# The order of a fused attention and Fourier-mixing kernel: a list scheduler's order replaced by a stored table

## The chip, the core and the metric

The kernel runs on one core of one Trainium2 chip. The metric is the device time of one execution in microseconds (us), as the median of three runs. The kernel before takes 950.33 us (949.66 to 951.9). Beside these runs stands one profiled execution with its trace; its durations are used in the working.

The core has five queues that run side by side, each strictly in its own order: the tensor engine (PE, with its weight loads PEld), the vector engine (DVE), the scalar engine (ACT), GpSimd (POOL) and the queue that issues most DMAs (SP). A step waits on semaphores for what it reads and for the buffers it writes, and everything behind it on its queue waits with it.

## What is computed

```
# q, k, v: 8 batches, 8 heads, 576 tokens, 64 wide; heads 0-3 a local mask (32 back), heads 4-7 a strided mask (every 32nd)
scores = scale * q @ k.T ; masked ; softmax ; attn @ v          -> x: [8, 576, 512]
X = fft(fft(x, axis=1), axis=2)
u = x + real(X)
un = (u - mean(u)) / sqrt(var(u) + 1e-6)                         # over the last axis
out = u + relu(un @ w_ch1) @ w_ch2                               # 512 -> 2048 -> 512
```

## The kernel before, in words

The work is cut into short steps written as Python generators (called threads here). A step yields an `op`: the engine it belongs to, an estimated duration, the buffers it takes and gives back (`get`, `put`) and the events it needs and sets. The class `Order` holds all open threads and picks, one after the other, the step that its cost model lets start first, with a priority (`bias`) for each kind of thread; then it lets that thread emit its instructions. So the result of `Order` is nothing but an order: the sequence in which instructions are put on each queue. Some steps may run on more than one engine (`alt`); `Order` chooses the engine too. While the two weight matrices are being read, `self.fill` puts small dummy matmuls on PE where the model sees a gap. `run` is called twice, once for the start (first batch of the attention, reading of the first weights) and once for the rest.

The threads, with the names used below (`b` is a batch, `hp` a pair of heads, so `5_2` is batch 5, pair 2; the pairs come in the order 2, 0, 1, 3):

- **Attention** (`att_pair`, lines 407 to 530): `load` (SP, L415 and L418), `sq` (ACT, L425 to L427, sums of squares of what was loaded), `total` (PE, L359), `scales` (DVE), `hi` and `lo` (ACT L446, DVE L461: split into two float16 halves), `vhi`, `vlo`, `scores` (PE, L484), `weigh`, `max`, `sub` (DVE, L813, L820, L822), `exp` (ACT), `wlo` (DVE, L500), `turn` (SP, a DMA transpose, L503), `pv` (PE, L515 or L522), `out` (DVE, L837 on), `xd` (SP, store to DRAM). Pairs 0 and 1 are local (tile `qk`), 2 and 3 strided (tile `pbt`).
- **Fourier mixing** (`fft_batch`), once per batch when its four `xd` have landed: `xa` (SP, a load, L893) and `xb` (POOL, four indirect gathers, L897), `O` and `E` (POOL, DVE, L907), `cosa` to `cosf`, `sin`, `SD`, `FH`, `FL` (split halves, ACT L920 and DVE L924 and L925), then the PE steps `A0`, `A2`, `A3` (L1015) with their evacuations `AH` (ACT, L1023) and `AL` (DVE, L1028), and `B0`, `B1`, `B2` (L1038) with `pq`, `rt`, `u`. `fcm` and the like come from `fscale`.
- **The two matrix products**, in 18 chunks `c` of 256 tokens: `st`, `rstd`, `un`, `uhi`, `ulo`, `uT` (normalise, split, transpose by DMA), eight `up c.n` (PE, L1387, 24 matmuls each), each followed by `relu c.n` (ACT, L1403 and L1404, tile `hb`, and `hf`, of which there is one) and `hlo c.n` (POOL, L1406), and eight `down c.n` (PE, L1427, 12 matmuls each, two half steps for n = 0), then two `fin c` (DVE, L1437), which free the two accumulators, and `store`. A `down c.n` needs `hlo c.n`; four hidden buffers go round.
- **The last three chunks** (15 to 17, class `Folded`) use sums of weight blocks. These are made in advance by `fold` (DVE, L1481), `fhi` (ACT, L1485) and `flo` (DVE, L1488, L1490) once the attention is over. Their PE steps are L1571 (`up`, `up2`, `up3`, `up4`) and L1714 (`down`), their vector steps `y11` (L1609), `y22`, `y12` (L1648), `s1` to `s4` (L1658), `hlo` (L1684).

PE runs two streams interleaved: the large `up` and `down` steps of one or two chunks, and between them the small steps of attention and Fourier mixing for later batches. The small PE results go to two PSUM buffers `big`, the `up` results to two buffers `ph`, the `down` results to two accumulators.

Of the kernel before, what the change touches and what calls it, by code (L numbers as in the profile page):

```python
# [19 lines left out]
B, H, S, D = 8, 8, 576, 64  # L20
# [3 lines left out]
    c=12.731, z=13.906, f0=-24.028, w0=-22.847, s0=-1.359, w1=3.314, s1=-5.983, p0=-26.912, p1=4.962, pn=-4.352,  # L24
# [141 lines left out]
class Op:  # L166
# [3 lines left out]
    def __init__(self, engine, dur, get="", put="", need="", sets="", at=None, lat=None, n=1, slack=0.0, dma=0.0, note="", alt=None):  # L170

        self.alt = {engine: (dur, 0.0), **{e: d if isinstance(d, tuple) else (d, AL) for e, d in alt.items()}} if alt else None
        self.engine, self.dur, self.at, self.n, self.slack, self.dma, self.note = engine, dur, at, n, slack, dma, note
        self.get = [g for g in get.split() if g[0] != "-"]

        self.put = put.split() + [g[1:] for g in get.split() if g[0] == "-"]
        self.need, self.sets = need.split(), sets.split()
        self.room = [(g, self.get.count(g)) for g in dict.fromkeys(self.get)]
        self.blocked = 0
        w = note.split()[0] if note else ""  # L180
        self.port = not w.startswith(PORT)
        self.lat = lat if lat is not None else {"S": 1.6, "T": 0.15}.get(engine, 0.1)


WT = {e: P["W" + e] for e in "SVAGT"}


class Order:


    def __init__(self):
        self.threads, self.free, self.room, self.events = [], dict.fromkeys("TVAGSDQ", 0.0), {}, {}
        self.waits = {}
        self.now = 0.0
        self.fill = None
        self.lock = 0.0, 0.0
        self.ring = []

    def free_events(self, e):
        self.events[e] = self.now  # L200
        for w in self.waits.pop(e, ()):
            w.blocked -= 1

    def spawn(self, gen, bias=None, at=None):
        th = [gen, self.bias if bias is None else bias, self.now if at is None else at, None]
        self.step(th, None)

    def step(self, th, end):
        try:
            o = th[3] = th[0].send(end)  # L210
            for e in o.need:
                if e not in self.events:
                    o.blocked += 1
                    self.waits.setdefault(e, []).append(o)
            if th not in self.threads:
                self.threads.append(th)
        except StopIteration:
            if th in self.threads:
                self.threads.remove(th)

    def run(self, part=False):
        while self.threads:
            best, cand = None, []
            for th in self.threads:
                o = th[3]
                if o.blocked:
                    continue
                t = th[2] if o.at is None else o.at
                ok = True
                for g, k in o.room:  # L230
                    r = self.room[g]
                    if len(r) < k:
                        ok = False
                        break
                    if r[k - 1] > t:
                        t = r[k - 1]
                if not ok:
                    continue
                for e in o.need:
                    if self.events[e] > t:  # L240
                        t = self.events[e]
                if o.alt:
                    o.engine = min(o.alt, key=lambda e: max(t, self.free[e]) + o.alt[e][0] + o.alt[e][1])
                    o.dur = o.alt[o.engine][0]
                est = max(t + o.slack, self.free[o.engine])
                if o.engine == "V" and o.port and o.dur and self.lock[0] <= est < self.lock[1] - 0.1:
                    est = self.lock[1] - 0.1
                if o.engine == "S" and o.dur:

                    est = max(est, self.free["D"] - 2.0)  # L250
                if o.engine == "A" and o.dma and len(self.ring) > 7:
                    est = max(est, self.ring[-8])
                cand.append((est, th))
                if best is None or est < best[0]:
                    best = est, o.engine
            if best is None and part:
                return
            if best is None:
                raise RuntimeError("stuck: " + str([(th[3].note, th[3].get, [e for e in th[3].need if e not in self.events]) for th in self.threads]))

            est, th = min((c for c in cand if c[1][3].engine == best[1] and c[0] <= best[0] + WT[best[1]]), key=lambda c: (c[1][1], c[0]))
            o = th[3]
            if o.engine == "T" and self.fill:
                n = int((est - self.free["T"] - 0.3) / 0.11)
                if n > 2:
                    self.fill(n)
            if o.engine == "S" and o.dur:
                self.free["S"] = est + 0.5 * o.n
                at = max(est + 1.3, self.free["D"])
                both = min(o.dur, max(0.0, self.free["Q"] - at))  # L270
                end = self.free["D"] = max(at + o.dur + both, est + 0.42 * o.n + 1.1)
                self.free["Q"] += both
            else:
                end = self.free[o.engine] = est + o.dur
                if o.engine == "G" and o.port and o.dur:
                    self.lock = est, end
                if o.dma and o.engine == "A":
                    at = max(est + 1.3, self.free["Q"])
                    both = min(o.dma, max(0.0, self.free["D"] - at))
                    end = self.free["Q"] = at + o.dma + both  # L280
                    self.free["D"] += both
                    self.ring.append(end + 1.3)
                elif o.dma:
                    end = self.free["D"] = max(est + 2.0, self.free["D"]) + o.dma
            for g in o.get:
                self.room[g].pop(0)
            self.now = th[2] = end + (o.lat if o.dur else 0)
            self.bias = th[1]
            self.step(th, self.now)
            for g in o.put:  # L290
                self.room[g] = sorted(self.room[g] + [self.now])
            for e in o.sets:
                self.events[e] = self.now
                for w in self.waits.pop(e, ()):
                    w.blocked -= 1


op = Op
# [3 lines left out]
def body(ctx: ExitStack, tc: tile.TileContext, a, out):  # L302
# [103 lines left out]
    def att_pair(b, hp):  # L406
# [41 lines left out]
        def values():  # L448
# [7 lines left out]
            V.scalar_tensor_tensor(out=lo, in0=src, scalar=sc[0:vp, 2:3], in1=hi, op0=ALU.mult, op1=ALU.subtract)  # L456

        spawn(values())
        yield op("V", 1.6, at=end - 0.65, put="" if local else "qk", note=f"lo {nm}")
        for hi, lo, src, f in parts:  # L460
            V.scalar_tensor_tensor(out=lo, in0=src, scalar=f, in1=hi, op0=ALU.mult, op1=ALU.subtract)  # L461
        if local:

            pb = qk.bitcast(F16)[:, 0 : 2 * NQB * 128].rearrange("p (x g c) -> p x g c", x=2, c=128)

            def pad():
                yield op("G", 0.5, sets=f"pad{nm}", note=f"pad {nm}")
                G.memset(pb[:, :, :, WIN:], 0.0)

            spawn(pad())  # L470
        else:
            pb = pbt
# [63 lines left out]
    def attended(b, hp):  # L536

        left.discard((b, hp))
        if left:
            return  # L540
        apool.release()
        pool = tail["pool"] = tc.alloc_tile_pool(name="tail", bufs=1, side="right", reuse_waits="tile")
        t = pool.tile([128, 25088], F16, name="tail")
        tail[0] = t[:, 0:16384].rearrange("p (n x d c) -> p n x d c", n=16, x=2, d=2)
        tail["t"] = t
        tail["hop"] = [hop(0), hop(1)]
        S_.room["hop"] = [S_.now] * 2
        tail["uTx"] = [t[:, 23552:25088].rearrange("p (n c) -> p n c", c=128)]
        S_.free_events("tail")
        S_.room["uTx"].append(S_.now)  # L550
        for q in range(4):
            spawn(folds(0, q), bias=P["tp"] + 0.1 * q)
            spawn(folds(1, q), bias=P["tp"] + 0.1 * q + 0.05)
# [1335 lines left out]
```

## Time and profile before

| | |
|---|---|
| runs | 950.33 us median of 3 (949.66 to 951.9) |
| profiled execution, first to last instruction | 946.9 us |
| PE busy | 910.9 us (96%) |
| DVE busy | 717.0 us (76%) |
| ACT busy | 506.2 us (53%) |
| POOL busy | 343.5 us (36%) |
| share of TensorE's full clock granted, mean | 0.986 |

The profile gives the span of the profiled execution and no separate time for it; the median of the runs lies 3.4 us above the span. A busy share is a sum over the whole span. Matmuls are pipelined, so PE counts as busy over short holes; a wait of PE is listed only where it stood idle. Times of day in the rows are us from the first instruction.

### The profile page before, as it was taken

Reading aid. Unit: us, or ns where it says so; the run is one execution under the profiler, and the core shown is the slowest. Engines: PE = TensorE matmul, PEld = TensorE weight load, DVE = VectorE, ACT = ScalarE, POOL = GpSimd, SP = SyncE. Lnnn points to the kernel's source line nnn. Section 1 sums busy time; section 2 is a strip of 40 time slices with the busy share of each in tenths; the row PEclk is TensorE's granted clock in tenths of the full one; section 3 lists DMA queues with packets and bytes.
Section 4 is the critical chain, followed back from the end, with each engine's and each line's share of the span. In section 5 each row is a group of like instructions: output and inputs, shape, how many; then the busy total and the mean of one; then the engine's idle time right before and its main releaser. Section 6 shows DMA issues by size and latency. Waiting matters only on the chain.

```text
span 946.9 us, 25320 instructions
## 1 busy us (share of the span) xinstructions
PE 910.9 (96%) x10597; PEld 668.4 (71%) x10599; DVE 717.0 (76%) x1342; ACT 506.2 (53%) x987; POOL 343.5 (36%) x315
## 2 busy tenths in 40 slices
PE   8778999999899999999999999999999999999997
PEld 6656885766666667665766677676666766689996
DVE  5988875678783896747956966697679889788675
ACT  4848874554653655643746564646423444365452
POOL 0240332245353631335325522552246256334000
PEclk9969999999999999999999999999999999999999
DMA  9788485363335635584445524625240102021100
GB/s 320 243 327 276 136 217 164 121 174 56 92 89 132 151 81 107 105 156 102 117 88 169 116 86 100 173 73 145 44 125 1 45 7 56 18 52 24 41 24 24
DMA packets 140371, 108.41 MB, mean 114 GB/s; under 512 B 108256, under 2 KB 118752, under 8 KB 140256
## 3 DMA queue, kind: packets, MB, share of 16 engines
q1 hardware_dynamic: 137696, 98.40, 38.7%
q0 software_dynamic: 2560, 8.39, 3.0%
q8 instruction: 83, 1.36, 0.6%
q14 instruction: 32, 0.26, 0.1%
HBM read 64.26 MB, written 18.89 MB: 88 GB/s over the span
## 4 chain that ended last, share of the span: by engine, by line
PE 77%; DMA 8%; DVE 7%; issue 3%; POOL 2%; ACT 2%; SPq 1%; DVEq 0%; POOLq 0%; ACTq 0%
PE acc L1427 28%; PE ph L1387 27%; PE acc L1714 5%; PE f L1571 2%; PE B L1038 2%; DMA xb<-xd,ridx 2%; DMA q<-in_w 2%; PE A L1015 1%; PE s L484 1%; DVE fold L1481 1%; PE o L515 1%; DMA W<-in_w 1%; DMA vn<-in_vl 1%; PE f_0x L1571 1%; DMA q<-in_qk 1%
## 5 line engine op out<-in xcount | busy, mean ns | idle before, releaser
L1387 PE MATMUL ph<-uT,W 128*128 128x256 f16 x2880 | 329.3, 273 | 1.2 <-DMA uT<-hb 1.2
L1387 PEld LDWEIGHTS <-W 128*128 128x128 f16 x2880 | 277.4, 98 | 42.8 <-DMA uT<-hb 1.4
L1427 PE MATMUL acc<-W,hb 128*128 128x512 f16 x1344 | 302.6, 379 | 1.5 <-DVE ub L1437 1.5
L1406 POOL TENSOR_TENSOR hb<-hf,hb 128x512 f16<-128x512 f32 x112 | 160.7, 1435 | 279.0 <-ACT hb L1404 196.5
L1427 PEld LDWEIGHTS <-hb 128*128 128x128 f16 x1344 | 129.2, 98 | 143.8 <-issue 1.7
L1403 ACT ACTIVATE hf<-ph 128x512 f32<-128x512 f32 x120 | 71.2, 593 | 180.7 <-PE ph L1387 113.1
L1404 ACT ACTIVATE hb<-ph 128x512 f16<-128x512 f32 x112 | 66.2, 591 | 0.0
L1481 DVE TENSOR_TENSOR fold<-fold,W 128x512 f32<-128x512 f32 x64 | 52.4, 847 | 0.3
L1714 PEld LDWEIGHTS <-tail 128*128 128x128 f16 x504 | 48.3, 98 | 5.3
L461 DVE SCALAR_TENSOR_TENSOR kt<-qk,sc,kt 128x576 f16<-128x576 f32 (+1 forms) x40 | 37.7, 982 | 3.3 <-ACT kt L446 3.1
L907 POOL TENSOR_TENSOR O<-xa,xb 128x1536 f32<-128x1536 f32 x8 | 33.5, 4189 | 16.0 <-DMA xb<-xd,ridx 12.4
L1161 POOL TENSOR_TENSOR rstd<-mv,negh 128x1 f32<-128x1 f32 x30 | 21.7, 730 | 44.0 <-DVE mv L1158 39.5
L1571 PEld LDWEIGHTS <-tail 128*128 128x128 f16 x576 | 34.7, 98 | 2.6 <-issue 1.4
L1658 POOL TENSOR_TENSOR hb<-hb 128x256 f32<-128x256 f32 x13 | 12.2, 950 | 65.4 <-DVE hb L1658 64.3
L1714 PE MATMUL acc<-fold,tail 128*128 128x256 f16 x288 | 35.0, 273 | 0.0
L446 ACT ACTIVATE kt<-qk,sc 128x576 f16<-128x576 f32 (+1 forms) x40 | 29.3, 784 | 10.1 <-DVE sc L402 9.0
L1140 ACT ACTIVATE pq<-B,fcm 128x128 f32<-128x128 f32 (+7 forms) x105 | 27.3, 380 | 11.5 <-PE B L1038 6.3
L1684 DVE TENSOR_TENSOR tail<-hb,tail 128x512 f16<-128x512 f32 (+1 forms) x47 | 31.8, 704 | 1.9 <-ACT tail L1681 1.5
L1681 ACT CAST tail<-hb 128x512 f16<-128x512 f32 (+1 forms) x48 | 25.6, 563 | 9.1 <-DVE hb L1658 5.5
L1179 DVE TENSOR_TENSOR unp<-un,unp 128x512 f16<-128x512 f32 x28 | 22.6, 806 | 9.1 <-ACT unp L1176 9.1
L1028 DVE SCALAR_TENSOR_TENSOR AT<-A,AT 128x290 f16<-128x290 f32 (+3 forms) x35 | 15.1, 479 | 18.8 <-ACT AT L1023 17.1
L897 POOL DMA_INDIRECT xb<-xd,ridx x24 | 26.7, 1111 | 7.3 <-issue 6.1
(313 smaller groups left out, 1550.9 us busy)
## 6 DMA issues: line engine op xcount, KB each, us to landing
qk<-in_qk SPq DMA_DIRECT2D x28, 592.0 KB
sa<-in_w SPq DMA_DIRECT2D x19, 512.0 KB
out<-ub SPq DMA_DIRECT2D x32, 256.0 KB
vn<-in_vl SPq DMA_DIRECT2D x10, 432.0 KB
W<-in_w SPq DMA_DIRECT2D x8, 512.0 KB
xd<-xo SPq DMA_DIRECT2D x16, 256.0 KB
xa<-xd SPq DMA_DIRECT2D x8, 512.0 KB
vn<-in_vs SPq DMA_DIRECT2D x10, 384.0 KB
```

The source lines that it names most:

```text
L446: A.activation(hi, src, AF.Copy, scale=f)
L461: V.scalar_tensor_tensor(out=lo, in0=src, scalar=f, in1=hi, op0=ALU.mult, op1=ALU.subtract)
L907: tt_ = lambda e, o, x, y, op: e.tensor_tensor(out=o, in0=x, in1=y, op=op)
L1387: T.matmul(ph[:, i, :], W1[:, 4 * (f0 // 512) + d, x, f0 % 512 : f0 % 512 + 128], self.uhl[y][:, d, :], start=(n == 0), stop=(n == 11))
L1403: A.activation(hf, ph, AF.Relu, scale=HS)
L1404: A.activation(hh, ph, AF.Relu, scale=HS)
L1406: G.tensor_tensor(out=hl, in0=hf, in1=hh, op=ALU.subtract)
L1427: T.matmul(self.acc[s], (hh, hl)[x][:, i, 128 * s : 128 * s + 128], W2[:, f, 1 - y, :], start=(f == 0 and n == 0), stop=(f == 15 and n == 2))
L1481: on(e).tensor_tensor(out=w, in0=w if x is None else x, in1=y, op=ALU.add if f else ALU.subtract)
L1571: T.matmul(dst[:, 128 * f : 128 * f + 128], w(x, i)[:, 128 * f : 128 * f + 128], u(y, i), start=opens and f == 0 and n == 0, stop=closes a ...
L1684: on(o).tensor_tensor(out=lo, in0=src, in1=hi, op=ALU.subtract)
L1714: T.matmul(dst, hop[:, x, j, 128 * i : 128 * i + 128], w(y, i), start=bank not in opened, stop=q == 3 and z in (6, 5, 3, 4) and i == 1 and ...
```

## The change

The list scheduler goes. `FIRST` and `SECOND` hold, for the two calls of `run`, the number of the thread that takes its next step (two digits in base 36), `SIDES` the engine for each step that has a choice, and `FILL` how many dummy matmuls stand before which step. The generators, and with them every instruction, its operands and its buffers' sizes, stay as they are.

```diff
+FIRST = (
+    "000m00000000000001000102000102000103020004040302050004030d060705030d060708060e0905080e09050f080a0a0d0f08080d0a0b"
...
+SECOND = (
+    "212424241g1h1i1j1g231l1g1h0r1o1g1i1h1g1h1x1i1i1j0r3z1h421l1i0r421j40441l1j1l451l1o1j431x1m461o47481x4b1o3z1k1n48"
...
+SIDES = (
+    "VVAVVAVAVVAAGVGVVGGAVVAVVAAVAVAVVAVAAVAAVAVAVAAVAAVVVAVAVAVVVVVAVVAAGVVGVGVVVVVVVVVVVVVVGVVGVGVVVVVVVGVVVVVVVVVV"
...
+FILL = {
+    8: 49, 17: 3, 39: 6, 47: 6, 55: 9, 63: 8, 70: 3, 77: 20, 85: 7, 89: 7, 103: 38, 119: 25, 124: 6, 162: 136, 263:
+    47, 415: 3, 1119: 6, 2148: 11
+}
...
     def spawn(self, gen, bias=None, at=None):
-        th = [gen, self.bias if bias is None else bias, self.now if at is None else at, None]
+        th = [gen, None]
+        self.threads.append(th)
         self.step(th, None)
...
-            est, th = min((c for c in cand if c[1][3].engine == best[1] and c[0] <= best[0] + WT[best[1]]), key=lambda c: (c[1][1], c[0]))
...
+        t = next(self.tables)
+        for i in range(0, len(t), 2):
+            th = self.threads[int(t[i : i + 2], 36)]
+            if th[1].alt:
+                th[1].engine = next(self.sides)
+            if self.fill and self.count in FILL:
+                self.fill(FILL[self.count])
+            self.count += 1
+            self.step(th, 0.0)
```

Read out by the generators, the two orders have the same 2,573 steps. `FIRST` is the list scheduler's order, every step with a choice has the engine it had, and the 370 dummy matmuls stand where they stood. What differs are places on the queues. Counted as what lies outside the longest common sequence, these are 68 of 551 steps on PE, 155 of 852 on DVE, 88 of 605 on ACT, 35 of 234 on POOL and 35 of 249 on SP. In the trace of before the first of them stands at 148 us and the last at 850 us. The places that the text below speaks of:

```
PE, batch 2   before: up 2.6, scores 3_0, up 2.7, A0 2, A2 2, down 2.4, A3 2, up 3.0
              after:  down 2.4, scores 3_0, up 2.6, up 2.7, A0 2, down 2.5, A2 2, up 3.0, A3 2
DVE           before: weigh 3_0, FL257 2, max 3_0, sub 3_0, AL0 2      after: weigh 3_0, max 3_0, sub 3_0, AL0 2, FL257 2
PE, batch 5   before: up 6.0, up 6.1, down 5.6, pv 4_1, scores 5_2, up 6.2, down 5.7, up 6.3, down 6.0, down 6.1, total 5_0,
                      up 6.4, up 6.5, down 6.2, pv 5_2, scores 5_0, up 6.6, down 6.3, down 6.4, up 6.7, down 6.5, up 7.0, down 6.6, pv 5_0
              after:  up 6.0, pv 4_1, up 6.1, down 5.6, scores 5_2, down 5.7, up 6.2, down 6.0, up 6.3, down 6.1, total 5_0,
                      down 6.2, up 6.4, up 6.5, up 6.6, pv 5_2, scores 5_0, down 6.3, down 6.4, up 6.7, down 6.5, up 7.0, down 6.6, pv 5_0
ACT           before: relu 6.2, exp 5_2, sq 5_0, relu 6.3               after: exp 5_2, sq 5_0, relu 6.2, relu 6.3
POOL          before: hlo 6.2, xb 4, hlo 6.3, O 4, hlo 6.4, hlo 6.5     after: xb 4, hlo 6.2, hlo 6.3, hlo 6.4, hlo 6.5, O 4
SP            before: uT 7_0, uT 7_1, xd 4_1, load 5_0, xa 4, turn 5_2  after: xd 4_1, uT 7_0, xa 4, load 5_0, uT 7_1, turn 5_2
PE, batch 6   before: up 8.4, up 8.5, pv 6_2, scores 6_0, down 8.2, down 8.3
              after:  down 8.2, down 8.3, up 8.4, scores 6_0, pv 6_2, up 8.5
POOL          before: O 5, hlo 8.4, pad 6_0                              after: hlo 8.4, pad 6_0, O 5
SP            before: xd 6_2, load 6_1, turn 6_0                         after: turn 6_0, xd 6_2, load 6_1
DVE, fin 13   before: fold, fold, fold, fold, fin 13, fin 13            after: fold, fold, fin 13, fold, fin 13, fold
DVE, chunk 15 before: hlo 15.0, hlo 15.0, y11 15.1                       after: hlo 15.0, y11 15.1, hlo 15.0
              before: ulo 16.3, fold, y12 15.1                           after: fold, ulo 16.3, y12 15.1
```

## Rows read from the trace of the kernel before

**Rows 1.** The page: the span, and busy time of each engine.
```profile
span 946.9 us, 25320 instructions
...
PE 910.9 (96%) x10597; PEld 668.4 (71%) x10599; DVE 717.0 (76%) x1342; ACT 506.2 (53%) x987; POOL 343.5 (36%) x315
```
**Rows 2.** Busy time by stretch: length, PE, PEld, DVE, ACT, POOL, granted clock, DMA, GB/s.
```profile
40.00:80.00 40.00, 32.54 (x290) 23.83 (x290) 33.27 (x56) 20.80 (x34) 15.24 (x11) 0.74 0.79 284
530.00:760.00 230.00, 230.00 (x2444) 160.22 (x2442) 180.91 (x331) 116.89 (x240) 88.51 (x83) 1.00 0.35 91
780.00:795.00 15.00, 14.77 (x112) 10.78 (x111) 14.80 (x18) 6.37 (x11) 10.67 (x10) 1.00 0.10 24
810.00:820.00 10.00, 10.00 (x76) 6.96 (x75) 6.26 (x10) 3.95 (x7) 2.31 (x2) 1.00 0.01 2
```
**Rows 3.** Waits of PE: line, releaser, us in total, times, longest.
```profile
PE A L1060 <- DVE FD L907: 5.5, 1, 5.5
...
PE o L522 <- DMA pT<-pbt: 3.1, 2, 2.2
...
PE acc L1427 <- DVE ub L1437: 1.5, 1, 1.5
...
PE f L1571 <- DVE raw L1609: 0.7, 1, 0.7
...
PE f_2x L1571 <- ACT raw L1619: 0.4, 1, 0.4
```
**Rows 4.** The chain that ended last: start, us, what.
```profile
250.45 2.62 PE ph L1387 x24
...
254.95 2.59 PE acc L1427 x12
```
**Rows 5.** Timeline, 241 to 254 us: start, us, instructions, idle before.
```profile
243.37 0.88 DVE L924 SCALAR_TENSOR_TENSOR FH<-O,fsc,FH 128x510 f16<-128x510 f32 x1 [0.22 <-ACT FH L920]
...
247.38 1.15 ACT L1023 ACTIVATE AT<-A 65x290 f16<-65x290 f32 x3
...
249.23 0.38 PE L1015 MATMUL A<-csin,FH 128*127 128x145 f16 x3 [2.69 <-DVE AT L1028]
```
**Rows 6.** Timeline, 404 to 432 us.
```profile
409.82 0.43 SPq L418 DMA_DIRECT2D vn<-in_vl  x1
...
416.88 1.16 ACT L427 ACTIVATE jk<-vn 96x1152 f16<-96x1152 f32 x1 [0.20 <-DMA vn<-in_vl]
...
419.23 1.15 POOL L1406 TENSOR_TENSOR hb<-hf,hb 128x512 f16<-128x512 f32 x1 [2.23 <-issue]
...
419.86 5.40 PE L1387 MATMUL ph<-uT,W 128*128 128x256 f16 x48
...
430.03 1.76 DVE L907 TENSOR_TENSOR E<-xa,xb 128x1536 f32<-128x1536 f32 x1 [3.62 <-DMA xb<-xd,ridx]
...
430.07 0.78 PE L522 MATMUL o<-vsx,pT 54*64 54x65 f16 x72 [2.21 <-DMA pT<-pbt]
```
**Rows 7.** Timeline, 436 to 452 us.
```profile
436.95 0.60 ACT L1403 ACTIVATE hf<-ph 128x512 f32<-128x512 f32 x1 [11.99 <-POOL hb L1406]
...
438.63 2.02 DVE L822 TENSOR_TENSOR sm<-sm,mx 128x864 f32<-128x864 f32 x1
...
450.32 1.06 PE L515 MATMUL o<-vlx,pT 96*64 96x65 f16 x54 [0.42 <-DMA pT<-qk]
```
**Rows 8.** Timeline, 787 to 798 us.
```profile
790.10 5.47 DVE L1481 TENSOR_TENSOR fold<-fold,W 128x512 f32<-128x512 f32 x4
...
795.50 1.40 DVE L1437 SCALAR_TENSOR_TENSOR ub<-acc,cout,ub 128x512 f32<-128x512 f32 x2
```
**Rows 9.** Timeline, 832 to 846.5 us.
```profile
833.82 2.19 DVE L1684 TENSOR_TENSOR tail<-hb,tail 128x512 f16<-128x512 f32 x2
...
843.34 0.43 DVE L1546 TENSOR_TENSOR unp<-un,unp 128x256 f16<-128x256 f32 x1 [1.25 <-ACT unp L1543]
843.68 0.68 DVE L1481 TENSOR_TENSOR fold<-W 128x512 f32<-128x512 f16 x1
```

More of the change, by code (lines that the diff above doesn't have):

```diff
@@ new lines @@
+SIDES = (
+    "VVAVVAVAVVAAGVGVVGGAVVAVVAAVAVAVVAVAAVAAVAVAVAAVAAVVVAVAVAVVVVVAVVAAGVVGVGVVVVVVVVVVVVVVGVVGVGVVVVVVVGVVVVVVVVVV"
+    "GVGVVGVVVVVVVVVVVVVVVVVGVVGVGVVVVVVVVVVVVVVVVVGVVGVGVVVVVVVVVVVVVVVVVGVGVVGVVVVVVVVVVVVVVVVVVVVVVVVVVVVGVVVVGVVV"
+    "VGVVVVVVVVVVVVVVVVVVVVVVVVVVVVVVVVVVVVVVGVVVVVVVVVGGGGVGGVVVVVVVVVGVVVVVVVVGVVGVVVGVVGGGVVVGVVVVVVGVVVVVVVVVGVGV"
+    "VGVGVVGVGVGVGVVVGVVVVVGVVGGVVVVVGVVVVVVVVVVVVVVVVVVVVVVVVVVVVVVVVGVVVVVVVGVVVVVVVGV"
+)
+FILL = {
+    8: 49, 17: 3, 39: 6, 47: 6, 55: 9, 63: 8, 70: 3, 77: 20, 85: 7, 89: 7, 103: 38, 119: 25, 124: 6, 162: 136, 263:
+    47, 415: 3, 1119: 6, 2148: 11
+}
@@ L188 @@
 class Order:
     def __init__(self):
[L192 to L197, printed above, removed]
+        self.threads, self.free, self.room, self.now, self.fill, self.count = [], dict.fromkeys("TVAGSDQ", 0.0), {}, 0.0, None, 0
+        self.tables, self.sides = iter((FIRST, SECOND)), iter(SIDES)
     def free_events(self, e):
-        self.events[e] = self.now
@@ L201, in free_events @@
-        for w in self.waits.pop(e, ()):
-            w.blocked -= 1
+        pass
     def spawn(self, gen, bias=None, at=None):
-        th = [gen, self.bias if bias is None else bias, self.now if at is None else at, None]
+        th = [gen, None]
+        self.threads.append(th)
         self.step(th, None)
@@ L209, in step @@
         try:
[L210 to L216, printed above, removed]
+            th[1] = th[0].send(end)
         except StopIteration:
-            if th in self.threads:
-                self.threads.remove(th)
+            th[1] = None
     def run(self, part=False):
[L222 to L259, printed above, removed]
-            est, th = min((c for c in cand if c[1][3].engine == best[1] and c[0] <= best[0] + WT[best[1]]), key=lambda c: (c[1][1], c[0]))
[L262 to L295, printed above, removed]
```

47 lines of the change are left out of this document (added).

## The prediction

> **What bounds the kernel now.** I read the page first. The span is 946.9 us and PE is busy for 910.9 us of it, 96%; the next engine, DVE, stands at 76% [rows 1]. The table by stretches says what that means for an order: between 530 and 760 us PE is busy for 230.00 of 230.00 us at full granted clock [rows 2]. A change that adds and removes no instruction cannot gain there. It can only take out time in which PE stands still, so the view that decides is the list of what PE waits for [rows 3], and the timelines around each of those waits. The largest entry, 5.5 us before A0 of the first batch (L1060), and the waits on the first weights lie before 148 us, where the first moved step stands; they stay. In the stretch of the moves, 148 to 850 us, PE is idle for more than 0.15 us at seven places only:
>
> A3 2 at 249 us, 2.69 [rows 5]; pv 5_2 at 430 us, 2.21 [rows 6]; pv 5_0 at 450 us, 0.42 [rows 7]; pv 6_2, the other wait of L522, 3.1 - 2.2 = 0.9; down 14.0 (L1427), 1.5; up2 15.1 (L1571), 0.7; up3 15.2 (f_2x), 0.4 [rows 3]. The sum is 8.8 us, 0.93% of the time. More than this the new order cannot give, apart from fractions of a tenth.
>
> **What the parts cost.** The table code runs on the host. No instruction is added or removed, no step changes its engine and the dummy matmuls stay where they are, so the change costs nothing by itself, and no cover hides anything here: the price is in the places alone. An up step of 24 matmuls takes 2.62 us of PE, a down step of 12 takes 2.59 [rows 4]; these are the units in which the PE steps move.
>
> A3 2 (2.69). It waits for a `big` buffer, freed by AL0 2. AL0 follows AH0, which began at 247.38 [rows 5] because ACT was busy with sq 3_1 and relu 2.7; PE had finished A0 some 4 us before. In the new order down 2.4 stands ahead of A0 and two steps stand between A0 and A3 (down 2.5, up 3.0) where one stood (down 2.4). Without its wait A3 stood at 249.23 - 2.69 = 246.54; it moves to 246.54 + 2.59 + 2.62 = 251.75. A0 is 2.6 us later too, but still over before AH0's turn on ACT comes, so the buffer is free at 249.2, as before. FL257 2, which A3 reads, goes behind AL0 on DVE: its first instruction is 0.88 long [rows 5] and the second about half, some 1.3 us, so it is done by 250.5. 1.2 us are left. All of the 2.69 goes.
>
> pv 5_2 (2.21). It waits for the DMA transpose of its weights, which landed at 430.07, together with the gather xb 4 (430.03) [rows 6]. Its place moves behind one more up step: 430.07 - 2.21 + 2.62 = 430.48, later than the landing. Besides, pv 4_1 moves ahead by two steps, 5.2 us, and with it its out and xd, which the gather of batch 4 waits for, and xb 4 no longer stands behind hlo 6.2 on POOL. The landing can only come earlier. All of the 2.21 goes.
>
> pv 5_0 (0.42). Its place relative to scores 5_0 comes one up step nearer, which alone would add 2.62. Against this stands the 11.99 us that relu 6.5 waited for POOL [rows 7]: O 4 stood ahead of hlo 6.4 and waited for the gather, hlo 6.4 held the only `hf`, relu 6.5 held ACT, cosa 4 stood behind it, cosd 4 behind that on DVE, and then sub 5_0, which began only at 438.63 and took 2.02. Now O 4 goes behind hlo 6.5 and cosb 4 ahead of weigh 5_0. I take the chain as at least 3 us shorter, so the 0.42 goes; the bounds are a gain of 0.42 and a loss of 2.62.
>
> pv 6_2 (0.9). It moves behind down 8.2, down 8.3, up 8.4 and scores 6_0 where up 8.4 and up 8.5 stood: 2 x 2.59 - 2.62 and a scores step of under 1 us, some 3.3 us later. It goes.
>
> down 14.0 (1.5). It waits for the accumulator that the first fin 13 frees. The two fin took 1.40 from 795.50, behind four folds of 5.47 in all, 1.37 each [rows 8]. With two folds fewer ahead of it, the first begins at 790.10 + 2.74 = 792.84 and ends at 793.5; PE arrives at about 794.8. It goes. What is late next are two folds and what follows them. DVE is full here (14.80 of 15 us), but busy for 6.26 of 10 us from 810 on [rows 2], so 2.7 us are made up there.
>
> up2 15.1 (0.7) and up3 15.2 (0.4). y11 15.1 now stands ahead of one of the two hlo of 2.19 / 2 = 1.1 us [rows 9]: more than 0.7. A fold of 0.68 fills the 1.25 in which DVE waited for ulo 16.3's input [rows 9], so y12 15.1 comes 0.68 sooner: more than 0.4. Both go.
>
> What the moves can cost. One new wait can be worked out. ACT now does sq 5_0 before relu 6.2, and down 6.2 comes two steps earlier on PE. The same PE steps as before stand ahead of it, so its place is 419.86, where up 6.4 stood [rows 6]. If the load behind sq 5_0 lands as it did (sq began its last part at 416.88), relu and hlo follow as relu 6.3 and hlo 6.3 did, and hlo ends at 419.23 + 1.15 = 420.38: a wait of 0.5 us. The load now stands behind xa 4 on SP and runs beside the gather; but xd 4_1, ahead of it, comes 5 us sooner. Bounds: 0, and, if the load lands only with the gather, the third rival's 13.7. I take 0.5, by the row of the same pair of steps.
>
> The other moved steps (the rest of 381) show no place where an input must come late: PE steps that move forward read a PE predecessor, or an hlo finished two steps earlier. But they use up spare time. Scores 4_1, for one, comes within about 1 us of lo 4_1, since total 4_1 moves behind an up step. On SP turn 6_0 goes ahead of xd 6_2 and load 6_1, which now wait for its vector step. For these I bound the cost by nothing and by as much as the old order has, 8.8, and take one further wait of the mean size of the seven, 8.8 / 7 = 1.3, because the margins found above are 1 us and more.
>
> Sum: 8.8 - 0.5 - 1.3 = 7.0. The terms come from the profiled execution with its span of 946.9; I carry them one to one to the median of 950.33, taking the 3.4 us outside the span as fixed: 950.33 - 7.0 = 943.3.
>
> By the Trainium skill, DMA: Bandwidth & Descriptors, section "Issuing engines are not separate DMA queues", DMAs run on the same 16 engines and interleave whatever engine issued them. The common landing of a transpose from SP and a gather from POOL at 430.0 agrees. By that rule load 5_0 is slowed by the gather beside it, which speaks for the first rival below.
>
> **Rivals.** *Part of it comes back.* The load takes engine time from the gather and the gather from it; its part for sq 5_0 came 416.88 - 409.82 = 7.06 us after its issue [rows 6], with the gather issued after it. If it lands 3 to 4 us later than before, down 6.2 waits 0.5 + 3.5 = 4, and the time is 950.33 - 8.8 + 4 + 1.3 = 946.8. For it: DMA is what ended the second and third wait. Against it: the earlier xd.
>
> *The waits only move.* If DVE and the landings set the pace and not the places on PE, new waits of about 8.8 us appear and the time stays at 950.3. For it: DVE at 14.80 of 15 us in one stretch. Against it: 180.91 of 230 us in the long one [rows 2].
>
> *Slower.* The load lands only with the gather, at 430.03. Then sq's last part, relu 6.2 and hlo 6.2 end at about 430.03 + 1.16 + 1.2 + 1.15 = 433.5, and PE stands at down 6.2 from 419.86 for 13.7 us. A wait of 5.5 us was followed by a mean granted clock of 0.74 from 40 to 80 us [rows 3, 2], where a stretch at the lower level cost up to 0.26 x 40 = 10.4 us. The time is 950.33 - 8.8 + 1.3 + 13.7 = 956.5, and up to 966.9 with the clock. It turns slower when this wait passes 8.8 - 1.3 + 1.9 = 9.4 us. Against it: large loads landed within some 7 us beside busy DMA.
>
> That the change does nothing is excluded: 68 places on PE differ.
>
> **How the numbers follow.** Forecast (941 to 946): 0.66. Part comes back (946 to 948.4): 0.21. The waits move (948.4 to 952.2): 0.09. Slower: 0.04. A difference under 0.2%, 1.9 us, is what a measurement of this kernel cannot tell from none; so faster 0.87, same 0.09, slower 0.04. The range begins at all seven waits gone and nothing new, 941.5, less the 0.7 by which a run lay under the median, and ends inside the second case: 940.8 to 948.2. The predicted time is 943.3.
>
> **What would show it.** In the list of PE's waits A L1015, o L522 and o L515, acc L1427 by fin, f and f_2x should be gone or under 0.2; PE's busy time stays at 910.9 within 1 us; the span falls by some 7 us to 940. New entries would stand at acc L1427 behind POOL's hb (down 6.2) or at n L359. The prediction is wrong if PE waits there for over 2 us, if the clock falls anywhere after 80 us, or if the seven waits come back under other names.

## The result: slower by 1.2%

The kernel after takes 961.99 us (median of 4 runs, 958.96 to 963.9); the kernel before, run beside it, 951.12 (949.66 to 952.17). The ratio is 1.0116 with a 95% interval of 1.0089 to 1.0143. The prediction was 943.3 us, with a range of 940.8 to 948.2 and a chance of 0.04 for slower: it missed, and on the wrong side.

The traces compared below are one execution each, and they lie further apart than the medians: 15.2 us in span, 10.9 us in time. In every run on record that gives both, the time lies 1.7 to 1.9 us above the span. So the profiled execution of before took some 948.7 us (an estimate, 946.9 + 1.8), less than any of the four timed beside after, and that of after, 963.9 us, is the slowest of its four: 4.3 us of the 15.2 are spread between executions. The 3.4 us that the prediction took as fixed outside the span were in part such spread.

The page of after, against [rows 1] of before: the span is 15.2 us longer, and PE is busy 7.5 us longer with the same matmuls, so part of the loss is matmuls that ran slower or came with holes between them, not only waits.

```profile
span 962.1 us, 25283 instructions
...
PE 918.4 (95%) x10599; PEld 671.1 (70%) x10599; DVE 714.1 (74%) x1342; ACT 505.5 (53%) x987; POOL 332.3 (35%) x315
```

The line numbers of after are 14 smaller (A L1015 is A L1001, and so on). The list of what PE waits for, to be held against [rows 3] (line, releaser, us in total, times, longest):

```profile
PE s L470 <- issue: 4.0, 9, 0.5
PE n L345 <- ACT jk L608: 3.4, 1, 3.4
...
PE n L345 <- ACT jk L413: 2.4, 1, 2.4
...
PE o L501 <- DMA pT<-qk: 2.2, 1, 2.2
...
PE A L1001 <- DVE FH L910: 1.2, 2, 1.0
PE ph L1373 <- issue: 1.0, 1, 1.0
```

The old entries are gone, as forecast: no A by DVE AT, no o by the transposes of 5_2, 5_0 and 6_2, no acc by fin. Six entries that before did not have stand in their place, 14.2 us in all. Two stretches at half of TensorE's clock come with them, the first two rows here (length, PE, PEld, DVE, ACT, POOL, granted clock, DMA, GB/s):

```profile
152.00:158.80 6.80, 5.97 (x19) 3.11 (x19) 0.00 (x0) 1.78 (x3) 1.02 (x1) 0.50 0.22 82
517.30:520.60 3.30, 2.86 (x18) 1.97 (x16) 1.73 (x4) 0.00 (x0) 0.70 (x1) 0.50 0.49 164
400.00:455.00 55.00, 55.00 (x598) 36.57 (x596) 37.26 (x73) 26.67 (x49) 24.89 (x24) 1.00 0.56 132
```

The last row is the place that the prediction feared most, down 6.2 and pv 5_2: PE is busy for 55.00 of 55.00 us there. The loss came elsewhere. Where, is read from the start of the same PE steps in the two traces, at points ahead of which both have done the same steps:

| step | before, us | after, us | later by | what lies in between, from the trace of after |
|---|---|---|---|---|
| up 1.5 | 177.91 | 184.66 | 6.8 | total 2_0 waits 3.37, half clock 6.8 long (3.4 lost) |
| up 2.1 | 211.61 | 220.22 | 8.6 | scores 3_2 takes 2.76 instead of 0.75; uT 2_1 is late (see the experiments) |
| up 4.0 | 302.21 | 308.70 | 6.5 | A3 2 no longer waits |
| up 6.0 | 397.22 | 405.38 | 8.2 | up 4.7 waits 0.97; scores 4_2 1.07 instead of 0.75 |
| up 8.0 | 496.97 | 502.86 | 5.9 | pv 5_2, pv 5_0 no longer wait; B2 4 waits 0.45 |
| up 9.0 | 541.95 | 552.07 | 10.1 | scores 6_2 takes 4.73 instead of 0.75; half clock 3.4 long (1.7 lost); pv 6_2 no longer waits |
| up 10.0 | 593.81 | 608.28 | 14.5 | A0 5 waits 0.95, total 6_1 2.38 |
| up 12.0 | 689.86 | 707.02 | 17.2 | pv 7_0 waits 2.23; scores 7_2 1.11 instead of 0.75 |
| up 16.0 | 851.60 | 866.83 | 15.2 | down 14.0 and chunk 15 no longer wait; 0.8 new |

Each new wait has its own story in the timelines. At total 2_0, which the new order puts ahead of the transposes 2_0 instead of behind pv 2_0:

```profile
147.71 0.33 SPq L601 DMA_DIRECT2D vlx<-in_v  x1
...
151.52 1.16 ACT L608 ACTIVATE jk<-vlx 96x1152 f16<-96x1152 f32 x1 [2.26 <-DMA vlx<-in_v]
...
152.82 0.16 PE L345 MATMUL n<-vsum,oneb 128*128 128x1 bf16 x1 [3.37 <-ACT jk L608]
...
154.56 4.88 PE L1413 MATMUL acc<-W,h 128*128 128x512 f16 x12
```

PE comes to the step 3.4 us before its input. The 12 matmuls of the down step behind it take 4.88 us where the same view of before has 2.75: that is the half clock. At total 6_1 the place on PE did not change; the load of its input did. In before it was issued on SP at 531.11 us, ahead of turn 6_0, and the part of sq 6_1 that reads it began 7.3 us later, without a wait:

```profile
531.11 0.44 SPq L418 DMA_DIRECT2D vn<-in_vl  x1
...
538.45 1.16 ACT L427 ACTIVATE jk<-vn 96x1152 f16<-96x1152 f32 x1
```

In after the same load stands behind turn 6_0 on SP (the transpose in the first row):

```profile
551.33 2.70 SPq L489 DMA_TRANSPOSE pT<-qk  x1
...
557.16 0.43 SPq L404 DMA_DIRECT2D vn<-in_vl  x1
...
565.23 1.16 ACT L413 ACTIVATE jk<-vn 96x1152 f16<-96x1152 f32 x1 [2.70 <-DMA vn<-in_vl]
```

At pv 7_0 it is the other way round, the transpose stands behind a load:

```profile
662.80 0.43 SPq L404 DMA_DIRECT2D vn<-in_vl  x1
663.35 5.00 SPq L489 DMA_TRANSPOSE pT<-qk  x1
...
671.90 0.28 PE L501 MATMUL o<-vlx,pT 96*64 96x65 f16 x6 [2.23 <-DMA pT<-qk]
```

At A0 5 a wait was moved, not removed. pv 6_2 was put behind two down steps and an up step so that PE would not wait for it. DVE, which in before took up its result without a wait (first row), now waits for it. From there to FH 5 DVE stands idle nowhere for more than 0.15 us, and FH 5 comes too late. This is read from the two timelines; it was not tried alone.

```profile
526.76 0.22 DVE L837 TENSOR_SCALAR rs<-o,sc 128x12 f32<-128x12 f32 x1
```
```profile
539.16 0.23 DVE L823 TENSOR_SCALAR rs<-o,sc 128x12 f32<-128x12 f32 x1 [6.46 <-PE o L508]
...
555.93 0.25 PE L1001 MATMUL A<-csin,FH 128*65 128x145 f16 x1 [0.95 <-DVE FH L910]
```

And scores 6_2 runs dry from within: no semaphore is named, 43 matmuls go in 0.53 us and the other 23 in groups of two to five, one group every 0.73 us, while POOL issues the four gathers of batch 5. Before (first row) had all 66 in 0.75 us:

```profile
510.13 0.75 PE L484 MATMUL s<-kt 64*64 64x54 f16 x66
```
```profile
513.41 0.53 PE L470 MATMUL s<-kt 64*64 64x54 f16 x43
514.25 0.25 PE L470 MATMUL s<-kt 64*64 64x54 f16 x5 [0.32 <-issue]
514.99 0.25 PE L470 MATMUL s<-kt 64*64 64x54 f16 x4 [0.48 <-issue]
...
517.89 0.25 PE L470 MATMUL s<-kt 64*64 64x54 f16 x2 [0.44 <-issue]
```
```profile
513.00 1.01 POOL L883 DMA_INDIRECT xa<-xd,ridx  x1 [0.15 <-issue]
514.32 0.96 POOL L883 DMA_INDIRECT xb<-xd,ridx  x1 [0.30 <-ACT vsx L440]
515.58 1.16 POOL L883 DMA_INDIRECT xb<-xd,ridx  x1 [0.30 <-issue]
517.04 0.95 POOL L883 DMA_INDIRECT xb<-xd,ridx  x1 [0.30 <-issue]
```

### The profile page after: what moved, and what is told of

It reads as the page before. It is cut to its first block, busy times and chain, and to the rows that moved or that the text cites. A ratio compares the mean times of both kernels' runs of the same rounds, so it can differ in the third digit from the quotient of the medians.

```text
span 962.1 us, 25283 instructions
## 1 busy us (share of the span) xinstructions
PE 918.4 (95%) x10599; PEld 671.1 (70%) x10599; DVE 714.1 (74%) x1342; ACT 505.5 (53%) x987; POOL 332.3 (35%) x315
## 5 line engine op out<-in xcount | busy, mean ns | idle before, releaser
L1392 POOL TENSOR_TENSOR hb<-hf,hb 128x512 f16<-128x512 f32 x112 | 154.4, 1379 | 303.7 <-ACT hb L1390 193.5
L447 DVE SCALAR_TENSOR_TENSOR kt<-qk,sc,kt 128x576 f16<-128x576 f32 (+1 forms) x40 | 33.7, 883 | 6.1 <-ACT kt L432 6.1
L893 POOL TENSOR_TENSOR O<-xa,xb 128x1536 f32<-128x1536 f32 x8 | 30.2, 3777 | 5.9 <-PE acc L1413 3.2
L1165 DVE TENSOR_TENSOR unp<-un,unp 128x512 f16<-128x512 f32 x28 | 25.2, 901 | 9.2 <-ACT unp L1162 8.5
L823 DVE TENSOR_SCALAR rs<-o,sc 128x12 f32<-128x12 f32 (+1 forms) x20 | 4.5, 226 | 36.4 <-PE o L508 28.1
L1667 ACT CAST tail<-hb 128x512 f16<-128x512 f32 (+1 forms) x48 | 25.8, 563 | 10.9 <-DVE hb L1644 8.2
L883 POOL DMA_INDIRECT xb<-xd,ridx x24 | 28.7, 1195 | 7.3 <-issue 5.8
```

Of the source, the lines that this page charges most:

```text
L893: tt_ = lambda e, o, x, y, op: e.tensor_tensor(out=o, in0=x, in1=y, op=op)
L1392: G.tensor_tensor(out=hl, in0=hf, in1=hh, op=ALU.subtract)
```

## The experiments

The theory after this reading: the seven waits were worth what the sum said, and a few moved steps that the prediction did not cost one by one lose more than twice that. The rivals: waits only move, so that what is mended in one place is lost in the next; and, for the gaps in the scores steps, the neighbour on PE, the traffic of the loads or the traffic of the gathers instead of their issuing. Each kernel uses the code of after with another table; the edits are written as orders of a queue. Ratios are to the kernel before, run beside each.

**One pair of steps put back, and the same pair moved alone.**

```diff
 PE:  down 0.2
-PE:  total 2_0
 PE:  turn 2_0, down 0.3, turn 2_0, down 0.4, pv 2_0
+PE:  total 2_0
-ACT: sq 2_0, copy 2_0
+ACT: copy 2_0, sq 2_0
```

> The new order with one pair of steps put back: on PE total 2_0 behind pv 2_0 again, on ACT sq 2_0 behind the first copy 2_0 again. If the time is lost where a step was put ahead of its input (first theory), the wait of 3.37 us at total 2_0 (149.46 us) goes and with it the 6.83 us at half clock that follow it (3.4 us): 962.0 - 6.8 = 955.2. If the clock stretch does not hang on that wait, 962.0 - 3.4 = 958.6. If DVE or the transfers set the pace and waits only move (rival), the time stays within 1 us of 962.0.

Measured: 957.64 us, ratio 1.0074 (1.0041 to 1.0107), so 4 us less than after by the ratios. In its trace up 1.5 stands at 179.42, 1.5 us behind before, of which 1.4 are there by down 0.2: the wait and the half clock behind it are gone together. The time by itself does not tell 955.2 from 958.6, since both lie inside the interval.

The opposite edit in the order of before, which is also the control that a table costs nothing:

```diff
 PE:  down 0.2
+PE:  total 2_0
 PE:  turn 2_0, down 0.3, turn 2_0, down 0.4, pv 2_0
-PE:  total 2_0
-ACT: copy 2_0, sq 2_0
+ACT: sq 2_0, copy 2_0
```

> The order of before, from a table, with one pair of steps moved as in the change: total 2_0 behind down 0.2 on PE, sq 2_0 ahead of the first copy 2_0 on ACT. It is also the control that a table costs nothing. First theory: a wait of 3.4 us at total 2_0 at about 149.5 us and some 6.8 us at half clock behind it, 951.1 + 6.8 = 957.9. Without the clock stretch 951.1 + 3.4 = 954.5. Rival, the time lost there is made up later because the attention of batch 2 is not what ends the stretch: within 1 us of 951.1.

Measured: 955.9 us, ratio 1.0051 (1.0028 to 1.0074): 4.8 us lost, 2.7 to 7.0 by the interval, so that the time by itself does not tell 3.4 from 6.8. In the trace PE waits 3.73 us at total 2_0:

```profile
156.67 0.16 PE L345 MATMUL n<-vsum,oneb 128*128 128x1 bf16 x1 [3.73 <-ACT jk L608]
```

The clock is at half for 3.4 us around the end of that wait, which cost 1.7; the wait plus that makes 5.4, and up 1.5 is 5.3 us later against down 0.2. The first theory holds; its 6.8 had the clock stretch at 6.8 us. Of the six traces with total 2_0 in the new place only that of after has this length; the other five have 3.4.

**Three scores steps back behind the up step.**

```diff
-PE:  scores 3_2, up 2.0
+PE:  up 2.0, scores 3_2
-PE:  scores 6_2, up 8.2
+PE:  up 8.2, scores 6_2
-PE:  scores 7_2, up 10.2
+PE:  up 10.2, scores 7_2
```

> The new order with three scores steps put back on PE behind the up step that stood ahead of them before: scores 3_2 behind up 2.0, scores 6_2 behind up 8.2, scores 7_2 behind up 10.2. Nothing else moves. First theory, the neighbour on PE matters: the gaps inside scores 3_2 (1.34 us) and scores 6_2 (2.67 us), the slow matmuls between them, and the 3.41 us at half clock (1.7 us) go; scores 3_2 and 6_2 take 0.75 us each as before instead of 2.6 and 4.2, so 962.0 - 1.9 - 3.5 - 1.7 - 0.3 = 954.6. Rival, the gaps come from the transfers running at the same time (the gathers of batches 2 and 5) and hit whatever small step stands there: time within 1.5 us of 962.0, gaps at about 214 and 515 us again or in a neighbouring small step.

Measured: 961.35 us, ratio 1.0106 (1.0068 to 1.0144): nothing gained. Scores 3_2 and 7_2 ran in 0.75 us, but scores 6_2 kept three gaps, and up 2.0 now showed a wait that the gaps of scores 3_2 had covered:

```profile
PE ph L1373 <- DMA uT<-unp: 2.8, 1, 2.8
```

Up 2.0 began at 217.68 us, 33.1 us behind up 1.5; in after it began at 217.59, 32.9 us behind it. So in after the gaps of scores 3_2 cost nothing themselves; uT 2_1 is what is late. The neighbour on PE is not what makes the gaps in scores 6_2.

**Two places on SP put back.**

```diff
-SP:  turn 6_0, xd 6_2, load 6_1, load 6_1
+SP:  xd 6_2, load 6_1, load 6_1, turn 6_0
-SP:  load 7_1, load 7_1, turn 7_0
+SP:  turn 7_0, load 7_1, load 7_1
```

> The new order with two places on SP put back: turn 6_0 behind load 6_1 again, and turn 7_0 ahead of load 7_1 again. First theory: total 6_1 waits 2.38 us because load 6_1 was issued at 557.2 us behind turn 6_0, and pv 7_0 waits 2.23 us because turn 7_0 stands behind load 7_1; both go, 962.0 - 4.6 = 957.4. Rival, the loads and transposes share the same transfer engines and only swap lateness: one of the two waits comes back at pv 6_0 or total 7_1 and the time is 959 to 962.

Measured: 960.1 us, ratio 1.0105 (1.0068 to 1.0141). The medians show only 2 us less than after, within the spread of the runs. The trace shows both waits gone and none in their place: from up 8.0 to up 12.0 it takes 200.24 us against 204.16 in after, 3.9 less.

**The gathers of batch 5, later, earlier, and beside an earlier scores step.**

```diff
-POOL: hlo 8.1, xb 5, hlo 8.2
+POOL: hlo 8.1, hlo 8.2, xb 5
```

> The new order with one step moved on POOL: the four gathers of batch 5 behind hlo 8.2, so they are issued some 8 us later, after scores 6_2; the loads on SP before and beside scores 6_2 stay. Theory, the gathers make scores 6_2 run out: no gap inside it, it takes 0.75 us instead of 4.2, and there is no stretch at half clock behind it; A0 5 waits longer since its gather is later (the 0.95 us grows by up to some 5 us), so the time is no measure here, 957 to 963. Rival, the traffic of the loads on SP makes it run out (they take 0.86 to 1.05 of the transfer engines from 512 to 518 us): the gaps stay between 513.9 and 518 us.

Measured: 956.47 us, ratio 1.0087 (1.0058 to 1.0117). Scores 6_2 runs through, and the clock stays at 1.00 from 506 to 516 us:

```profile
509.87 0.75 PE L470 MATMUL s<-kt 64*64 64x54 f16 x66
```

The loads on SP filled the transfer engines as before (1.03 of their time in the first us of the step and 1.05 in the next, the same as in after). From up 8.0 to up 9.0 it takes 44.35 us against 49.21 in after. The traffic of the loads is excluded. A0 5 did not wait longer either, 0.58 against 0.95.

```diff
-PE:   scores 6_2, up 8.2
+PE:   up 8.2, scores 6_2
-POOL: hlo 8.1, xb 5, hlo 8.2
+POOL: xb 5, hlo 8.1, hlo 8.2
```

> The new order with two places changed: scores 6_2 behind up 8.2 (as in the run that put three scores steps back, where three gaps of 0.47 to 0.49 us stayed in it), and on POOL the gathers of batch 5 ahead of hlo 8.1, some 4 us earlier. The issuing of the gathers is then over before scores 6_2 begins at about 516 us, while the data of the gathers still move (12 to 80% of the transfer engines). If what counts is that POOL is issuing gathers: no gap, the step takes 0.75 us, no stretch at half clock behind it; hlo 8.1 is 3 us later, which down 8.1 does not feel; 962.0 - 5.1 = 957. If it is the moving of the gathers' data: gaps of 0.5 us again inside the step, 960 to 962.

Measured: 958.81 us, ratio 1.0086 (1.0062 to 1.011). Scores 6_2 began at 513.82, 2 us after the last gather was issued, and took 0.75 us with the engines of the transfers full (1.06 in its first us, 0.12 of it the gathers' data):

```profile
513.82 0.75 PE L470 MATMUL s<-kt 64*64 64x54 f16 x66
```

The same place on PE had three gaps with the gathers beside it. So it is the issuing on POOL, not the moving of data.

```diff
 the order of before
-PE:   up 8.2, scores 6_2
+PE:   scores 6_2, up 8.2
```

> The order of before with one PE step moved: scores 6_2 ahead of up 8.2 instead of behind it, 2.6 us earlier, at about 507.4 us. In before the four gathers of batch 5 are issued on POOL from 505.1 to 510.5 us, and the step began at 510.1 without a gap. Theory, small matmuls run out while POOL issues gathers: gaps of 0.3 to 0.5 us inside the step from about 508 us until about 510.5, the step takes about 3.4 us instead of 0.75, 950.8 + 2.7 = 953.5, and 1.7 more with a stretch at half clock. Rival, the gaps of the new order come from something else there (its loads, its buffers): no gap, time within 1 us of 950.8.

Measured: 949.72 us, ratio 0.9995 (0.9974 to 1.0016), no gap: this expectation missed. The step ran from 511.67 to 512.42, across the end of one gather (510.80 to 512.14) and the pause before the next (512.44). Over the fourteen traces, no scores step of this kind (66 matmuls) that met no gather took more than 0.86 us; of 28 that met one, 19 took 0.98 to 4.73 us, and nine stayed at 0.75 to 0.81, some of them with up to 0.74 us of overlap. Gathers being issued are needed for the gaps; what else decides in a case, and what the gathers take from PE, stays open. The run also bounds what a table by itself costs: apart from this one step it has the order of before, and the times agree within 0.3%.

**Three stretches of the new order alone.** The order of before with the new one in 211 to 296, 392 to 486 and 690 us to the end.

```diff
 the order of before
+the new order of the steps that before has at 211 to 296 us       (A3 2)
+the new order of the steps that before has at 392 to 486 us       (pv 5_2, pv 5_0)
+the new order of the steps that before has from 690 us on         (fin 13, chunk 15)
```

> The order of before, with the new order in three stretches only: around A3 2 (211 to 296 us of before), from pv 4_1 to pv 5_1 (392 to 486 us) and from 690 us to the end. These hold six of the seven waits that the prediction wanted gone (all but pv 6_2, 0.9 us). If the seven waits were rightly priced and the loss comes from the other moved steps (first theory): A3 2 2.69, pv 5_2 2.21, pv 5_0 0.42, down 14.0 1.5, up2 15.1 0.7, up3 15.2 0.4 go, and the 0.3 and 0.5 us new at 850 us come: 950.8 - 7.1 = 943.7. Rival, waits only move: 949 to 952.

Measured: 943.37 us, ratio 0.9935 (0.9911 to 0.996): 0.3 us from what was expected, and faster than before by 6.2 us. What is left of PE's waits there:

```profile
PE acc L1700 <- DVE tail L1670: 0.5, 1, 0.5
PE B L1024 <- ACT pq L1126: 0.4, 1, 0.4
...
PE f L1557 <- ACT raw L1591: 0.3, 1, 0.3
PE o L508 <- DMA pT<-pbt: 0.3, 1, 0.3
...
PE A L1001 <- DVE FH L910: 0.2, 1, 0.2
```

**The other way round: the new order with the losing stretches undone.**

```diff
 the new order
-the new order of the steps that before has at 147 to 211 us
-the new order of the steps that before has at 486 to 582 us
-SP:  load 7_1, load 7_1, turn 7_0
+SP:  turn 7_0, load 7_1, load 7_1
```

> The new order with the old one put back in two stretches (147 to 211 us: total 2_0, uT 2_1, scores 3_2; 486 to 582 us: scores 6_2, A0 5, total 6_1, and with them the 0.9 us at pv 6_2 again), and turn 7_0 ahead of load 7_1 again on SP. First theory, the loss sits in these places alone: from the profiled execution of the new order 9.4 us by up 2.0, 8.6 us from up 8.0 to up 10.0 and 2.2 us at pv 7_0 go: 962.0 - 20.2 = 941.8; by the profile it is faster than before by 950.8 - 941.8 = 9.0 us. Rival, waits only move: 949 us or more.

Measured: 944.0 us, ratio 0.9939 (0.9915 to 0.9963). The rival is excluded, but the gain is 5.8 us (3.5 to 8.1 by the interval), short of the 9.0 expected; the 20.2 of the expectation came from the two traces, which lie 4.3 us further apart than the medians. The two halves meet: the order of before with the gaining stretches and the new order without the losing ones come out within 0.7 us of each other.

**Five and six steps put elsewhere.** The expectation counts 369 moved steps; the numbers given with the change add up to 381. The edits at total 2_0, at the two transposes and at the late gathers of batch 5, in one kernel:

```diff
 the new order
-PE:   total 2_0 ahead of the transposes 2_0;  ACT: sq 2_0 ahead of copy 2_0
+PE:   total 2_0 behind pv 2_0;                ACT: sq 2_0 behind copy 2_0
-SP:   turn 6_0 ahead of load 6_1, turn 7_0 behind load 7_1
+SP:   turn 6_0 behind load 6_1, turn 7_0 ahead of load 7_1
-POOL: xb 5 ahead of hlo 8.2
+POOL: xb 5 behind hlo 8.2
```

> The new order with five of its 369 steps put elsewhere: total 2_0 on PE and sq 2_0 on ACT back, turn 6_0 and turn 7_0 on SP back, the gathers of batch 5 on POOL behind hlo 8.2. First theory: 6.5 us by total 2_0 (wait and clock), 4.6 by the two turns, some 5 by scores 6_2 and the clock stretch behind it go, the 0.95 us at A0 5 stays: 962.0 - 16.1 = 945.9, 0.5% faster than before. Left are uT 2_1 at 212 us (some 2.6), up 4.7 (1.0) and A0 5. Rival, waits move on: 950 or more.

Measured: 948.48 us, ratio 0.9968 (0.9952 to 0.9985): faster than before by 0.3%, 2.6 us short of the expectation. By the ratios the five steps give back 1.5% of the time. The largest rest is at up 2.1, 2.7 us behind before, of which 0.6 are there by down 0.2. One operation of scales 3_2 holds DVE there, and with it ulo 2_1 and the transpose that up 2.0 needs. In after:

```profile
207.43 2.71 DVE L387 TENSOR_SCALAR ib<-ib 128x3 int32<-128x3 int32 x1
...
210.59 0.68 DVE L1165 TENSOR_TENSOR unp<-un,unp 128x512 f16<-128x512 f32 x1
```
```profile
207.34 1.16 POOL L1392 TENSOR_TENSOR hb<-hf,hb 128x512 f16<-128x512 f32 x1 [0.73 <-DMA xd<-xo]
208.44 1.38 POOL L328 MEMSET pbt<- 128x1536 f16 x1
```

In before the same operation came when POOL's fills were over:

```profile
203.44 0.17 DVE L401 TENSOR_SCALAR ib<-ib 128x3 int32<-128x3 int32 x1
```

So two more kernels, each with the five edits:

```diff
-DVE:  scales 3_2, ulo 2_1
+DVE:  ulo 2_1, scales 3_2
-PE:   scores 3_2, up 2.0
+PE:   up 2.0, scores 3_2
```

> The kernel with five steps put elsewhere, and two more: scales 3_2 on DVE behind ulo 2_1 instead of ahead of it, and scores 3_2 on PE behind up 2.0. In the new order one of the tiny operations of scales 3_2 took 2.71 us on DVE (0.17 in before) while POOL filled tiles, and ulo 2_1, and with it the transpose uT 2_1 that up 2.0 needs, came that much later. Theory, up 2.0 is late by uT 2_1, and scores 3_2 with its gaps only fills the same time: with both put back up 2.0 begins some 2.7 us earlier than in the run with five steps and neither gap nor wait is left there, 948.5 - 2.7 = 945.8. Rival: the 2.71 us is a hold of POOL that hits whatever DVE does then, ulo 2_1 itself; uT 2_1 stays late, up 2.0 waits 2 to 3 us and the time stays at 948 to 949.

```diff
-DVE:  scales 3_2, ulo 2_1
+DVE:  ulo 2_1, scales 3_2
```

> The same without the move of scores 3_2: only scales 3_2 behind ulo 2_1 beside the five steps. Theory of two layers: uT 2_1 is early, but scores 3_2 stands ahead of up 2.0 and still runs out beside the gathers of batch 2 (three gaps, 2.8 us instead of 0.75), so up 2.0 begins no earlier than in the run with five steps less some 0.5 us: 948 to 948.5. If the gaps cost nothing or come from uT 2_1: 945.8.

Measured: 945.12 us, ratio 0.9959 (0.9941 to 0.9978), and 945.07 us, ratio 0.994 (0.992 to 0.9959). The theory of uT 2_1 had 2.7 us for the place on DVE. Against the kernel with five steps (0.9968) the ratios give 0.9 and 2.7 us, with intervals that overlap, and the medians, each against before beside it, 2.2. The traces are sharper: from down 0.2 to up 2.1 it takes 67.1 us with five steps, 65.0 and 65.3 in these two, and 64.9 in before. The theory of two layers was wrong for the second kernel: scores 3_2, still ahead of up 2.0, took only 1.09 us. With DVE free earlier its place against the gathers had moved as well; it met the last 0.1 us of one and the beginning of the next. The tiny operation took 0.99 us and stood behind ulo 2_1:

```profile
200.79 1.23 DVE L1165 TENSOR_TENSOR unp<-un,unp 128x512 f16<-128x512 f32 x1 [0.68 <-ACT unp L1162]
201.94 0.15 DVE L386 TENSOR_SCALAR ib<-n 128x3 int32<-128x3 int32 x1
202.12 0.99 DVE L387 TENSOR_SCALAR ib<-ib 128x3 int32<-128x3 int32 x1
```

With six of its steps put elsewhere the new order beats before by 0.6%. The kernel with the three stretches has the lowest ratio, 0.9935, but the two intervals overlap almost wholly.

## Why the prediction was wrong, step by step

**The seven waits, 8.8.** Right. All are gone in after. The six that were tested alone were worth 7.1 by the sum (7.9 less the 0.8 new in chunk 15) and 6.2 by the ratio (interval 3.8 to 8.4). For A3 2, 0.22 us of waiting for FH was left where 1.2 us of margin was claimed; at B2 4 and in chunk 15 small new waits of 0.45, 0.3 and 0.5 appeared that were not forecast.

**Down 6.2, 0.5.** No wait there at all (55.00 of 55.00 us). The first and third rival both hung on this load. By the Trainium skill, DMA: Bandwidth & Descriptors, section "Issuing engines are not separate DMA queues", DMAs run on the same 16 engines and interleave, whatever engine issued them. From this the prediction took it that the load is slowed by the gather; if it was, PE did not feel it.

**"The other moved steps (the rest of 381) show no place where an input must come late", 1.3.** This step failed. Its term was to be 1.3, with 8.8 as its bound; by the table above it is 15.2 + 7.2 = 22 us, where 7.2 is what the falling rows take back with the 0.9 of pv 6_2 (2.1 + 2.3 + 1.9 + 0.9). With the medians' 10.9 in place of the traces' 15.2 it is still 18. It went wrong in four ways.

- *It was a sentence and not a working.* "PE steps that move forward read a PE predecessor, or an hlo finished two steps earlier" is false for total 2_0, which reads sq 2_0 on ACT. The trace of before had both numbers:

```profile
147.68 0.33 SPq L615 DMA_DIRECT2D vlx<-in_v  x1
...
151.43 1.16 ACT L622 ACTIVATE jk<-vlx 96x1152 f16<-96x1152 f32 x1
```

  If sq 2_0 keeps its time it ends, with the 0.19 us that reads its sum out, at about 152.8. The new place of total 2_0 on PE is at 149.3. That is a wait of 3.5 us; 3.37 came.
- *A named risk was not followed.* "On SP turn 6_0 goes ahead of xd 6_2 and load 6_1, which now wait for its vector step": in before that load was issued 7.3 us before the part of sq 6_1 that reads it; behind the transpose it came 26 us later by the time of day (531.11 and 557.16), 10 of them the general delay, and total 6_1 waited 2.38. Turn 7_0 was not looked at.
- *What is late next was asked at down 14.0, and not at pv 6_2.* For pv 6_2, "It goes" was right; DVE then waited 6.46 us for the same step, and A0 5 paid 0.95.
- *A lower clock was priced only for the wait at down 6.2.* "If the clock falls anywhere after 80 us" was named as a sign of being wrong. It fell twice, which cost 3.4 + 1.7 = 5.1 us, a third of the net loss in the traces.

**What could not be read from before.** The gaps in scores 6_2 (4 us, and the clock behind them). In before the same step met only the last 0.34 us of a gather and took 0.75, so no row had this price. The hold of 2.71 us on an operation that takes 0.17 is another matter. Before has five such operations of 0.87 to 1.15 us, each of them beside an add on POOL and over when POOL's work is. One of them:

```profile
466.92 1.15 DVE L401 TENSOR_SCALAR ib<-ib 128x3 int32<-128x3 int32 x1
```

That scales 3_2 would meet an add with five fills behind it could not be read there.

**The rivals.** "The waits only move" fell: two waits swap place at pv 6_2 and A0 5, but where the losing steps are put back the loss goes and does not return elsewhere (944.0, 945.1). "Slower" had the right mechanism, a long new wait with a lower clock behind it, at the wrong place and with a chance far too small: of 381 moved steps only those beside the seven waits had been costed, and the 8.8 taken as the bound of the rest came from the old waits, not from the new places.

## What to carry to other kernels

An order is judged step by step: for every step that moves forward on a queue, the end of each of its inputs on the other queues stands in the old trace, and here one input that ended 3.4 us after the new place cost more than any two of the waits removed gave back. When a step moves back to spare one engine a wait, the next to look at is who reads its result. A table that loses need not be wrong as a whole: compare the start of the same steps in both traces, undo the places where the difference jumps up, and keep those where it falls.

## What the runs showed of the hardware

**Runs of tiny matmuls starve beside gathers.** While POOL issued indirect gathers, a step of 66 small matmuls with their weight loads took up to 4.73 us instead of 0.75, in groups of two to five every 0.73 us with no semaphore named. Without a gather beside it no such step took more than 0.86. Large matmuls beside the gathers show no such gaps: of the 2,517 of the up and down steps that began while a gather was being issued, in the fourteen traces, one stood behind a gap, and that one waited for a named transpose. A similar gap of 0.7 to 1.3 us at up 4.7, right behind the 72 small matmuls of pv 4_2, stood in four of the ten traces with the new order there, with no gather within 25 us of it; its cause was not tried.

**The clock after a wait.** Around the end of the waits at total 2_0 (3.0 to 4.0 us) the granted clock fell to 0.5 every time, for 3.4 us in five traces and 6.8 in that of after. Behind the old wait at A3 2 it fell with 2.68 and 2.70 us in two experiments and not with 2.69 in before; behind the waits of 2.21 to 2.58 us from 148 us on it never did, and behind those of 2.61, 2.82 and 2.85 us (three scores steps back) and 3.73 us (scores 6_2 early) it did each time. It also fell with no wait above 0.51 us, behind the gaps inside scores 6_2 in after and two experiments, and behind those inside scores 3_2 in one. One such stretch of 3.4 us costs 1.7 us.

**Work on POOL holds a tiny DVE operation.** It took 2.71 us instead of 0.17, from the beginning of a POOL add to the end of the fills behind it, and 0.99 us when it began beside a fill. In the fourteen traces this operation never took more than 0.17 us when POOL had no work beside it (134 times); beside POOL's work it was held in some cases and not in others, and what decides was not tried. The Trainium skill, SBUF — State Buffer, section "Who interferes with whom", lists tensor_scalar among the operations that can contend with GpSimd for a shared pair of ports, and says that the one that comes second is blocked for the whole instruction of the first. The trace agrees in that the hold ends with POOL's work; but 2.71 us is longer than any one of the POOL instructions beside it (1.38 at most).
